# A single filler as 256 keys of both heads in one PSUM bank, with a TensorE wait between its halves, and singles at the units' first steps

## The chip, the cores and the metric

One Trainium2 chip, one core. The metric is device time of one execution in microseconds. The kernel before takes 1504.08 us in the median of three runs (1503.17 to 1506.13).

## The reference

Two attentions over the same x (2048 rows, width 512), mixed row by row by a gate:

```python
g = _sigmoid((x * gate_w).sum(-1, keepdims=True))
a = _A_ref(x, A_wqkv, A_wo)            # 32 heads of 16, each row sees 8 rows, 2 apart, up to itself
b = _B_ref(x, B_wq, B_wk, B_wv, B_wo)  # 32 query heads of 16, one key and value head, all rows
return g * a + (1 - g) * b
```

B is the long part. Its weights B_wq and B_wk are scaled by 8, so its scores are large, and the softmax needs the true maximum of each query's 2048 scores before it takes exponentials.

## The kernel before

**Units and steps.** B is cut into 32 units of 512 queries and 4 heads (`NQB` x `NHG`). A unit has 16 steps, one for each 128 keys, and step `s` of the main loop (lines 1106 to 1155) belongs to unit `s // 16`; `kt` is the step within the unit. A step does this:

- `exp_pair` (L468) twice: two score matmuls (L473), one head on the lower 64 rows of the TensorE array and one on the upper 64, into the two banks of `eb[0]` or `eb[1]` (`pe` in the profile), and one exponential by ScalarE (L475) of the 128 x 1024 scores.
- `weighted` (L480): four heads' exponentials of the step before times the values, into the bank `po` (L483), on all 128 rows.

**Fills.** The maxima come from a second pass over the same scores, spread between the steps of earlier units: for each of a unit's 8 groups of 128 queries and head pairs, and each quarter of the keys (512), two matmuls of 62 rows (`max_mm`, L324) and a maximum over the keys by VectorE into the tile `mx`. The list `slots` holds these items in order; an item counts as two halves, one a head, and a unit has `NF // NU` = 64 of them. `filled` (L329) counts a unit down; at zero it reduces `mx` once more (L334) and sends the maxima to the rows 62 and 63 of the unit's queries, so the scores that the exponentials see are already shifted.

- A **pair** (`fill_pair`, L339) does an item at once: two matmuls into the two banks of `m2` (`pm` in the profile), one reduction of 128 x 1024 (L344).
- A **single** (`fill_one`, L348) does half an item, one head: one matmul of 512 keys into the bank `m1` (`ps`), one reduction of 128 x 512 (L355).

**Order.** The order on every engine is the order in which the Python code emits instructions. It is steered by a planner: `clk` is its time on TensorE, ScalarE and VectorE, `free` the time at which each bank is free, `T_R` to `T_TTR` (L45) its costs, `after` (L86) adds one. In a step the usual order is first scores, pair, single, second scores, weighted sum. `fill_ready` (L853) takes a fill if its bank is free by the planner's clock; `singles(s)` (L849) lets singles in while the pairs of the steps ahead can't do the rest; singles are left out at a unit's first step (`kt` zero, L1145), where `finish_a` (L495) also has VectorE transpose `po` (L497). Where a unit's maxima would come too late, `pause` (L863) does fills with the exponentials' banks while no step goes on.

**Around it.** Before the main loop, the projections run with fills between them (`stream`, L689). Three times `out_phase` (L728) projects four output rows of 128; the last four are done by the generator `spread` (L776): its matmuls (L812) go into `m2`, four pairs a step, once all fills are done, and each row's sum is taken out by ScalarE (L829) and VectorE (L831) into `parts`. After the last step the tail (L1163 to L1188) normalises the last unit, multiplies it by its part of the output weights and adds `parts`. GpSimd computes attention A and sets the `mx` tiles.

Of the kernel before, what the change touches and what calls it, by code (L numbers as in the profile page):

```python
# [13 lines left out]
P = 128  # L14
# [34 lines left out]
def gated_mix_kernel(ctx, tc, xt, wa, wk, wq, wo_a, wo_b, out):  # L49
# [20 lines left out]
    def home(v):  # L70

        return (v % NB, v - NB) if v < 2 * NB - 2 else ((v - NB) % (NB - 2), v - NB + 2)
# [13 lines left out]
    def after(eng, ready, dur):  # L86
        clk[eng] = max(clk[eng], ready) + dur
        return clk[eng]
# [213 lines left out]
    half = []  # L302
# [4 lines left out]
    def fillable():  # L307
        return bool(half) or bool(slots) and slots[0][0] < len(stacked) and stacked[slots[0][0]] <= clk["pe"]

    def unit_tile(v):  # L310
        for x in (v, v + 1) if pe else (v,):
            if x < NU and x not in left:
                mx[x] = wp.tile([P, 2, 2, 4, 4], F32, name="mx", bufs=3)
                if pe:
                    nc.gpsimd.memset(mx[x], -FMAX)
                    charge(250)
                else:
                    nc.scalar.activation(mx[x].rearrange("p b i t k -> p (b i t k)"), ident[:, 0:64], AF.Identity, scale=0.0, bias=mk[:, 6:7])
                left[x] = NF // NU
        return mx[v]  # L320
# [3 lines left out]
        nc.tensor.matmul(dst, qst[home(v)[0]][b:b + 62, pr, t * P:(t + 1) * P], kst[b:b + 62, kc * 512:(kc + 1) * 512], start=True, stop=True)  # L324

    def to_go():
        return 2 * len(slots) + len(half)

    def filled(v, n):  # L329
        left[v] -= n  # L330
        if not left[v]:
            ms = wp.tile([P, 2, 2, 8], F32, name="ms")
            m = mx.pop(v).rearrange("p b i t k -> p b (i t) k")
            nc.vector.tensor_reduce(ms, m.unsqueeze(2).to_broadcast([P, 2, 2, 8, 4]), AX.X, ALU.max)  # L334
            mt = wp.tile([P, 32], F32, name="mt")
            nc.vector.transpose(mt, ms.rearrange("p b x y -> p (b x y)"))
            tasks.append((after("dve", 0, 0.66) + (2.0 if kcd and not pe else 0.1), shift_a, (v, mt)))

    def fill_pair(dst, key):  # L339
        v, pr, t, kc = slots.pop(0)  # L340
        m = unit_tile(v)
        for odd in range(2):
            max_mm(dst[:, odd, :], v, pr, t, kc, odd)
        nc.vector.tensor_reduce(m[:, :, pr, t, kc], dst, AX.X, ALU.max)  # L344
        free[key] = after("dve", after("pe", 0, T_R) + T_LAT, T_RED2) + 0.08
        filled(v, 2)

    def fill_one(dst=m1, key="m1"):  # L348
        if not half:
# [115 lines left out]

    pe, pexp, exped = [], {}, {}

    def exp_pair(s, pr, other=False):  # L468
        bank, key = (m2, "m2") if other else (eb[pr], f"e{pr}")
        u, kt = divmod(s, NJ)  # L470
        for odd in range(2):
            b = 64 * odd
            nc.tensor.matmul(bank[:, odd, :], kst[b:b + 64, kt * P:(kt + 1) * P], qst[home(u)[0]][b:b + 64, pr, :], start=True, stop=True)  # L473
        e = px.tile([P, 2, 512], F32, name="pexp", bufs=6)
        nc.scalar.activation(e, bank, AF.Exp, scale=SCALE)  # L475
        free[key] = after("act", after("pe", free[key], T_R) + T_LAT, T_EXP)
        exped[s] = free[key]
        pexp[s, pr] = e

# [296 lines left out]
    def spread(js, n):  # L776

        m = 3 * (C + n)

        def turn_all(j):  # L780
            bank = m1
            for c in range(C):
                nc.tensor.transpose(bank[:, c * P:(c + 1) * P], oa[c // 2][:, j, c % 2 * P:(c % 2 + 1) * P], ident)
            after("pe", 0, 0.7)
            own = p2[0].tile([P, C, P], F32, name="raw", bufs=1)
            nc.scalar.activation(own, bank.rearrange("p (c q) -> p c q", c=C), AF.Copy)
            after("act", clk["pe"] + T_LAT, 0.6)
# [12 lines left out]
        parts_a(js[0], turn_all(js[0]))  # L800
        yield 3.0
        while slots or half:
            yield 1.0
        for j in js:
            nxt = j + 1 if j != js[-1] else None
            items = []
            for i in range(m):
                items = items or out_items(j, n)
                st, mv = items[i]
                for b in range(2):  # L810
                    h = slice(64 * b, 64 * b + 64)
                    nc.tensor.matmul(m2[:, b, :], st()[h], mv[h], start=(i == 0), stop=(i == m - 1))  # L812
# [16 lines left out]
            nc.scalar.activation(parts[j], m2[:, 1, :], AF.Copy)  # L829
            after("dve", after("act", clk["pe"] + T_LAT, 0.5), 0.7)  # L830
            nc.vector.tensor_add(parts[j], m2[:, 0, :], parts[j])  # L831
            if nxt:
                parts_a(nxt, raw)
            yield 1.5
        done.add("last")

    def spread_some(k):
# [13 lines left out]
        return 2 * max(0, 16 * (NU - 1) - 16 - s) + PER_ROW * max(0, NJ - 4 - outs) < to_go()  # L851

    def fill_ready(key, slack):  # L853
        if fillable() and free[key] <= clk["pe"] + slack:
            clk["pe"] = max(clk["pe"], free[key])
            if key == "m1":
                fill_one()
            elif half and (not slots or half[0][0] < slots[0][0] or slots[0][0] >= len(stacked)):
                fill_one(m2[:, 0, :], "m2")
            elif slots:  # L860
                fill_pair(m2, "m2")

    def pause(most):  # L863
        n = 0
        while n < most and slots and fillable():
            key = min(("e0", "e1", "m2"), key=lambda k: free[k])
            clk["pe"] = max(clk["pe"], free[key])
            if half:
# [191 lines left out]
    def done_mm(at):  # L1060
# [45 lines left out]
    for s in range(NS + 1):  # L1106
# [11 lines left out]
        v = min(x[0][0] for x in (half, slots, [(NU,)]) if x)  # L1118
# [4 lines left out]
        order = (0, "m2", "m1", 1) if s > 1 else (1, "m2", 0, "m1") if s else ()  # L1123
        k, n = outs // 4, C - (outs >= NJ - 4)
        if outs == NJ - 4:
            if NU - 3 in shaped and not half and not singles(s) and not later_rows and "last" not in done:
                later_rows.append(spread(list(range(outs, NJ)), n))
            if short > 0 and steps < 2:
                pause(short)
# [8 lines left out]
        elif short > 0 and steps < 2:  # L1138
            pause(short)

        for which in order:
# [18 lines left out]
    assert not slots and not half and not hooks and not tasks and "last" in done, (len(slots), len(hooks), len(tasks), outs)  # L1160


    for x in range(8):  # L1163
# [2 lines left out]
    for x in range(2):  # L1166
# [51 lines left out]
```

## Time and profile before

| | us |
|---|---|
| median of the runs | 1504.08 |
| the profiled execution | 1503.76 |
| its span | 1502.0 |
| TensorE busy | 1479.2 |
| ScalarE busy | 1285.7 |
| VectorE busy | 1188.4 |
| GpSimd busy | 1024.8 |

How to read the lines below: in the timeline, the columns are the start in us from the span's start, the time, the engine, the kernel's line, the operation, the tiles written and read, their shapes and how many instructions are merged in the row; in brackets stands the engine's idle time before it and what ended it. PE is TensorE's matmuls, PEld its weight loads, DVE is VectorE, ACT ScalarE, POOL GpSimd. In a row of groups, "| 196.8, 398 |" is the busy time in us and the mean of one in ns. In a row of windows the stretch and its length come first, then busy time and (count) of the line asked for; in a row for all engines these stand for PE, PEld, DVE, ACT and POOL in this order; the granted TensorE clock (1.00 is full) follows. A matmul's row runs from its start to the modelled arrival of its last column; the next one on the same rows can start before that end.

### The profile page before, as it was taken

To read this page: it belongs to the slowest core of one execution; us is meant where nothing else is said; L and a number is where in the kernel's file an instruction comes from. 1 tells how busy PE (TensorE), PEld (TensorE's weight loads), DVE (VectorE), ACT (ScalarE), POOL (GpSimd) and SP (SyncE) were. 2 spreads that over 40 slices of the span, in tenths; PEclk is the share of its full clock that TensorE was granted. 3 is DMA by queue.
4 is the path that set the end of the run, shared out by engine and by line. 5 is a ranking of instruction groups with operands and counts; after the bars stand their busy time and mean duration, and the time that the engine had idled before them with its cause. 6 is when DMAs were issued, how large, how long until landed. Compare 5 with 4: busy or idle time off the path is not lost.

```text
span 1502.0 us, 29449 instructions
## 1 busy us (share of the span) xinstructions
PE 1479.2 (98%) x11020; PEld 710.5 (47%) x11020; DVE 1188.4 (79%) x1814; ACT 1285.7 (86%) x1672; POOL 1024.8 (68%) x1806
## 2 busy tenths in 40 slices
PE   9999999999999999999999999999999999999998
PEld 6899888433333333333733345333333463333343
DVE  6976666788888888888788888888888888888801
ACT  5568988899999999999899988999989889999785
POOL 7876988788888888988988799788897130111021
PEclk9999999999999999999999999999999999999999
DMA  6754223121120211211212112021120000000000
GB/s 219 212 147 143 76 87 117 33 83 46 60 84 12 73 58 41 70 41 41 69 41 70 41 41 87 12 70 41 41 76 16 12 30 12 2 1 2 1 2 28
DMA packets 44287, 87.75 MB, mean 58 GB/s; under 512 B 9520, under 2 KB 25952, under 8 KB 39920
## 3 DMA queue, kind: packets, MB, share of 16 engines
q1 hardware_dynamic: 37136, 46.89, 10.3%
q0 software_dynamic: 6432, 37.94, 7.5%
q8 instruction: 86, 1.41, 0.4%
q10 hardware_dynamic: 576, 1.05, 0.2%
q14 instruction: 57, 0.47, 0.1%
HBM read 59.02 MB, written 26.30 MB: 57 GB/s over the span
## 4 chain that ended last, share of the span: by engine, by line
PE 91%; ACT 5%; DVE 2%; issue 1%; DMA 0%; POOL 0%; SPq 0%; DVEq 0%; ACTq 0%; POOLq 0%
PE po L483 33%; PE pe L473 25%; PE pe L1057 8%; PE pm L324 8%; PE ps L324 5%; PE pe L740 4%; PE pm L409 2%; ACT dd L419 2%; ACT pexp L475 1%; PE ps L409 1%; PE pm L812 1%; PE po L409 1%; PE pe L183 1%; DMA xraw<-xt 0%; DVE mx L344 0%
## 5 line engine op out<-in xcount | busy, mean ns | idle before, releaser
L475 ACT ACTIVATE pexp<-pe 128x1024 f32<-128x1024 f32 x1021 | 987.3, 1023 | 106.0 <-PE pe L473 103.6
L344 DVE TENSOR_REDUCE mx<-pm 128x2 f32<-128x1024 f32 x508 | 620.0, 1221 | 147.4 <-PE pm L324 139.6
L483 PE MATMUL po<-pexp,vst 128*32 128x512 f32 x4096 | 546.6, 606 | 0.0
L473 PE MATMUL pe<-qst,kst 64*128 64x512 f32 x1914 | 520.4, 455 | 5.6 <-DVE mx L344 2.9
L473 PEld LDWEIGHTS pe<-qst,kst 64*128 64x128 f32 x1914 | 213.3, 184 | 424.6 <-ACT pexp L475 410.2
L355 DVE TENSOR_REDUCE mx<-ps 128x1 f32<-128x512 f32 x446 | 303.1, 680 | 2.1 <-PE ps L324 2.1
L324 PE MATMUL pm<-kst,qst 62*128 62x512 f32 x968 | 196.8, 398 | 2.9 <-DVE mx L344 2.1
L543 POOL TENSOR_TENSOR pr<-aext 128x256 f32<-128x256 f32 x256 | 182.6, 741 | 3.4 <-DMA aext<-ad 3.1
L324 PE MATMUL ps<-kst,qst 62*128 62x512 f32 x422 | 177.3, 420 | 0.5 <-DVE mx L355 0.3
L603 POOL TENSOR_TENSOR oa<-oa,av 128x256 f32<-128x256 f32 x224 | 164.5, 734 | 14.9
L483 PEld LDWEIGHTS po<-pexp,vst 128*32 128x32 f32 x4096 | 80.6, 108 | 174.5 <-issue 166.6
L600 POOL TENSOR_TENSOR av<-aext,lg 128x256 f32<-128x256 f32 x224 | 139.7, 623 | 12.5
L324 PEld LDWEIGHTS ps<-kst,qst 62*128 62x128 f32 x422 | 77.5, 184 | 68.3 <-DVE mx L355 64.9
L1057 PE MATMUL pe<-wah,xl 64*128 64x384 f32 (+1 forms) x504 | 108.9, 338 | 0.0
L419 ACT ACTIVATE dd<-pm 128x512 f32<-128x512 f32 x166 | 92.0, 608 | 19.6 <-PE pm L409 9.5
L1057 PE MATMUL pe<-wah,xh 64*128 64x384 f32 (+1 forms) x504 | 108.6, 337 | 0.0
L1057 PE MATMUL pe<-wal,xh 64*128 64x384 f32 (+1 forms) x504 | 108.3, 337 | 0.0
L429 DVE CUSTOM_DVE_ANT_0 dd<-ps,dd 128x512 f32<-128x512 f32 x83 | 57.4, 692 | 58.4 <-PE ps L409 25.4
L324 PEld LDWEIGHTS pm<-kst,qst 62*128 62x128 f32 x968 | 93.2, 187 | 8.0 <-DVE mx L344 3.4
L509 POOL TENSOR_TENSOR rl<-rl,gate_t 128x16 f32<-128x16 f32 x31 | 6.9, 222 | 118.2 <-DVE rl L503 118.1
L549 POOL TENSOR_TENSOR tr<-pr 128x512 f32<-128x512 f32 x64 | 81.7, 1277 | 4.1
L549 POOL TENSOR_TENSOR tr<-tr 128x256 f32<-128x256 f32 (+1 forms) x128 | 72.5, 567 | 9.0
(215 smaller groups left out, 1908.1 us busy)
## 6 DMA issues: line engine op xcount, KB each, us to landing
aext<-ad POOLq DMA_DIRECT2D x32, 1056.0 KB, 5.5
ad<-stage SPq DMA_DIRECT2D x32, 384.0 KB
qst<-qd SPq DMA_DIRECT2D x60, 128.0 KB
xraw<-xt SPq DMA_DIRECT2D x16, 256.0 KB
qd<-qhi SPq DMA_DIRECT2D x16, 256.0 KB
qd<-qlo SPq DMA_DIRECT2D x16, 256.0 KB
qst<-qd SPq DMA_DIRECT2D x60, 64.0 KB
qst<-ml SPq DMA_DIRECT2D x216, 2.0 KB
```

Source lines behind the costliest of these rows:

```text
L324: nc.tensor.matmul(dst, qst[home(v)[0]][b:b + 62, pr, t * P:(t + 1) * P], kst[b:b + 62, kc * 512:(kc + 1) * 512], start=True, stop=True)
L344: nc.vector.tensor_reduce(m[:, :, pr, t, kc], dst, AX.X, ALU.max)
L355: nc.vector.tensor_reduce(m[:, odd, pr, t, kc:kc + 1], dst, AX.X, ALU.max)
L419: nc.scalar.activation(dd[0][:, odd], m2[:, odd, :], AF.Abs)
L473: nc.tensor.matmul(bank[:, odd, :], kst[b:b + 64, kt * P:(kt + 1) * P], qst[home(u)[0]][b:b + 64, pr, :], start=True, stop=True)
L475: nc.scalar.activation(e, bank, AF.Exp, scale=SCALE)
L483: nc.tensor.matmul(po[32 * i:32 * i + 32, :], vst[:, kt, :], pexp[s, i // 2][:, i % 2, :], start=(kt == 0), stop=(kt == NJ - 1))
L543: nc.gpsimd.tensor_mul(pr[:, k], q, e[:, o:o + NH, AC:2 * AC])
L549: nc.gpsimd.tensor_add(nx, cur[:, :, 0:n], cur[:, :, n:2 * n])
L600: nc.gpsimd.tensor_mul(av, e[:, o:o + NH, 2 * AC:].rearrange("p j (h d) -> p j h d", d=DH), lg[:, w].unsqueeze(3).to_broadcast([P, NH, AG, ...
L603: nc.gpsimd.tensor_add(ao, ao, av)
L1057: nc.tensor.matmul(front[2 if x == last else x % 2][0][:, b, :n], l[h], r[h], start=(i == 0), stop=(i == 3 * C - 1))
```

## The change

- A single becomes 256 keys of **both** heads in the one bank `m1` (`fill_apart`): even head in columns 0 to 255, odd head in 256 to 511. The two matmuls use different halves of the array and the same bank. They stand around the second pair of scores of the step: first half on the lower rows, the scores of the odd head (upper rows), the scores of the even head (lower rows), then an instruction without work that waits until the first half is in the bank, then the second half on the upper rows. One reduction takes both maxima.
- Since an item has then two quarters of keys in one place of `mx`, a second tile `mb` takes the upper 256 keys; it is set by GpSimd as `mx` is, and `filled` joins the two with one `tensor_max`. An item begun so is ended by a second such single or by `fill_rest`, which does 256 keys of both heads in `m2` or in another pair of banks.
- Singles are let in at the units' first steps. Where half an item is open, or an item's unit has no `mb`, the old form stays.
- The planner counts 0.2 us more for scores with such a single, where before the single had `T_R` (0.23).
- `spread` may begin with up to 9 halves left; between its rows VectorE alone empties `m2`; the last row's add stands behind the first transposes of the tail, and one subtraction of the tail goes from GpSimd to VectorE. At the end of the projections a stretch without new pairs (`ended`) begins four matmuls sooner.

```diff
     def unit_tile(v):
-        for x in (v, v + 1) if pe else (v,):
+        for x in (v, v + 1):
...
                 if pe:
+                    mb[x] = pe[0].tile([P, 2, 2, 4, 4], F32, name="mb", bufs=3)
+                    nc.gpsimd.memset(mb[x], -FMAX)
+                    charge(250)
...
     def to_go():
-        return 2 * len(slots) + len(half)
+        return 2 * len(slots) + len(half) + len(quarter)
...
-            m = mx.pop(v).rearrange("p b i t k -> p b (i t) k")
+            m = mx.pop(v)
+            if v in mb:
+                nc.vector.tensor_max(m, m, mb.pop(v))
+            m = m.rearrange("p b i t k -> p b (i t) k")
...
+    def fill_apart(scores):
+
+        if not quarter:
+            v, pr, t, kc = slots.pop(0)
+            quarter.extend([(v, pr, t, kc, 0), (v, pr, t, kc, 1)])
+        v, pr, t, kc, x = quarter.pop(0)
+        m = mb[v] if unit_tile(v) is not None and x else mx[v]
+        ks = slice(kc * 512 + x * 256, kc * 512 + x * 256 + 256)
+        for odd in range(2):
+            b = 64 * odd
+            if odd:
+                scores(1)
+                scores(0)
+                nc.tensor.keepalive_nop([nc.tensor.lower_ap(m1[:, 0:256])])
+            nc.tensor.matmul(m1[:, 256 * odd:256 * odd + 256], qst[home(v)[0]][b:b + 62, pr, t * P:(t + 1) * P], kst[b:b + 62, ks], start=True, stop=True)
+        nc.vector.tensor_reduce(m[:, :, pr, t, kc], m1.rearrange("p (b k) -> p b k", b=2), AX.X, ALU.max)
+        filled(v, 1)
...
-    def exp_pair(s, pr, other=False):
+    def exp_pair(s, pr, other=False, apart=False):
...
+        if apart:
+            fill_apart(scores)
+        else:
+            scores(0)
+            scores(1)
         e = px.tile([P, 2, 512], F32, name="pexp", bufs=6)
         nc.scalar.activation(e, bank, AF.Exp, scale=SCALE)
-        free[key] = after("act", after("pe", free[key], T_R) + T_LAT, T_EXP)
+        at = after("pe", free[key], T_R + 0.2 * apart)
+        free[key] = after("act", at + T_LAT, T_EXP)
+        if apart:
+            free["m1"] = after("dve", at + T_LAT, T_RED1) + 0.08
...
-            nc.scalar.activation(parts[j], m2[:, 1, :], AF.Copy)
-            after("dve", after("act", clk["pe"] + T_LAT, 0.5), 0.7)
-            nc.vector.tensor_add(parts[j], m2[:, 0, :], parts[j])
             if nxt:
+                nc.vector.tensor_copy(parts[j], m2[:, 1, :])
+                nc.vector.tensor_add(parts[j], m2[:, 0, :], parts[j])
                 parts_a(nxt, raw)
-            yield 1.5
+                after("dve", clk["pe"] + T_LAT, 1.4)
+                yield 1.5
+            else:
+                nc.scalar.activation(parts[j], m2[:, 1, :], AF.Copy)
...
-        if x == last - 1 and i == 3 * C - 2:
+        if x == last - 1 and i == 3 * C - 6:
             ended.add(1)
...
-            if NU - 3 in shaped and not half and not singles(s) and not later_rows and "last" not in done:
+            if NU - 3 in shaped and to_go() <= 9 and not later_rows and "last" not in done:
                 later_rows.append(spread(list(range(outs, NJ)), n))
...
             elif which == "m1":
-                if not later_rows and (kt or not s) and singles(s):
-                    fill_ready("m1", M1S)
+                if not later_rows and singles(s):
+                    if half or slots and not quarter and slots[0][0] in left and slots[0][0] not in mb:
+                        fill_ready("m1", M1S)
+                    elif (quarter or fillable()) and free["m1"] <= clk["pe"] + M1S and s < NS:
+                        apart = True
             elif s < NS:
-                exp_pair(s, which % 2 or which // 2, which == 2)
+                if apart and which:
+                    clk["pe"] = max(clk["pe"], free["m1"])
+                exp_pair(s, which % 2 or which // 2, which == 2, apart and which > 0)
...
-        nc.gpsimd.tensor_sub(tl[:, 1], own, tl[:, 0].bitcast(F32))
+        (nc.vector if x else nc.gpsimd).tensor_sub(tl[:, 1], own, tl[:, 0].bitcast(F32))
         tls.append(tl)
+        if not x:
+            nc.vector.tensor_add(parts[NJ - 1], m2[:, 0, :], parts[NJ - 1])
```

More of the change, by code (lines that the diff above doesn't have):

```diff
@@ L301, in gated_mix_kernel @@
     slots += [(v, pr, t, kc) for v in range(2, NU) for pr in range(2) for t in range(4) for kc in range(4)]
-    half = []
+    half, quarter, mb = [], [], {}
     free = {"m2": 0.0, "m1": 0.0, "e0": 0.0, "e1": 0.0, "po": 0.0}
@@ L346, in fill_pair, with fill_rest @@
         filled(v, 2)
+    def fill_apart(scores):
[14 more added lines that the diff above has]
+        filled(v, 1)
+    def fill_rest(dst, key):
+        v, pr, t, kc, x = quarter.pop(0)
+        m = mb[v] if x else mx[v]
+        for odd in range(2):
+            b = 64 * odd
+            c = kc * 512 + x * 256
+            nc.tensor.matmul(dst[:, odd, 0:256], qst[home(v)[0]][b:b + 62, pr, t * P:(t + 1) * P], kst[b:b + 62, c:c + 256], start=True, stop=True)
+        nc.vector.tensor_reduce(m[:, :, pr, t, kc], dst[:, :, 0:256], AX.X, ALU.max)
+        free[key] = after("dve", after("pe", 0, T_R) + T_LAT, T_RED1) + 0.08
+        filled(v, 1)
     def fill_one(dst=m1, key="m1"):
@@ L466, in gated_mix_kernel, with scores @@
     pe, pexp, exped = [], {}, {}
-    def exp_pair(s, pr, other=False):
+    def exp_pair(s, pr, other=False, apart=False):
         bank, key = (m2, "m2") if other else (eb[pr], f"e{pr}")
         u, kt = divmod(s, NJ)
-        for odd in range(2):
+        def scores(odd):
             b = 64 * odd
             nc.tensor.matmul(bank[:, odd, :], kst[b:b + 64, kt * P:(kt + 1) * P], qst[home(u)[0]][b:b + 64, pr, :], start=True, stop=True)
+        if apart:
[3 more added lines that the diff above has]
+            scores(1)
         e = px.tile([P, 2, 512], F32, name="pexp", bufs=6)
         nc.scalar.activation(e, bank, AF.Exp, scale=SCALE)
-        free[key] = after("act", after("pe", free[key], T_R) + T_LAT, T_EXP)
+        at = after("pe", free[key], T_R + 0.2 * apart)
+        free[key] = after("act", at + T_LAT, T_EXP)
+        if apart:
+            free["m1"] = after("dve", at + T_LAT, T_RED1) + 0.08
         exped[s] = free[key]
@@ L801, in spread @@
         yield 3.0
-        while slots or half:
+        while slots or half or quarter:
             yield 1.0
@@ L853, in fill_ready @@
     def fill_ready(key, slack):
-        if fillable() and free[key] <= clk["pe"] + slack:
+        if (fillable() or quarter) and free[key] <= clk["pe"] + slack:
             clk["pe"] = max(clk["pe"], free[key])
@@ L857, in fill_ready @@
                 fill_one()
+            elif quarter and (later_rows or not slots or quarter[0][0] < slots[0][0]):
+                fill_rest(m2, "m2")
             elif half and (not slots or half[0][0] < slots[0][0] or slots[0][0] >= len(stacked)):
                 fill_one(m2[:, 0, :], "m2")
-            elif slots:
+            elif slots and fillable():
                 fill_pair(m2, "m2")
@@ L864, in pause @@
         n = 0
-        while n < most and slots and fillable():
+        while n < most and (quarter or slots and fillable()):
             key = min(("e0", "e1", "m2"), key=lambda k: free[k])
             clk["pe"] = max(clk["pe"], free[key])
+            if quarter:
+                fill_rest({"e0": eb[0], "e1": eb[1], "m2": m2}[key], key)
+                n += 1
+                continue
             if half:
@@ L1117, in gated_mix_kernel @@
                     assert pause(4)
-        v = min(x[0][0] for x in (half, slots, [(NU,)]) if x)
+        v = min(x[0][0] for x in (half, quarter, slots, [(NU,)]) if x)
         need = left.get(v, NF // NU)
@@ L1139, in gated_mix_kernel @@
             pause(short)
+        apart = False
         for which in order:
@@ L1159, in gated_mix_kernel @@
         run_pool()
-    assert not slots and not half and not hooks and not tasks and "last" in done, (len(slots), len(hooks), len(tasks), outs)
+    assert not slots and not half and not quarter and not hooks and not tasks and "last" in done, (len(slots), len(hooks), len(tasks), outs)
     for x in range(8):
```

## The prediction

> **What bounds the kernel now.** I read the page's first line, the busy shares and the chain that ended last; then the timeline of single steps of the main loop; then counts by stretch.
>
> ```profile
> span 1502.0 us, 29449 instructions
> PE 1479.2 (98%) x11020; PEld 710.5 (47%) x11020; DVE 1188.4 (79%) x1814; ACT 1285.7 (86%) x1672; POOL 1024.8 (68%) x1806
> ...
> PE 91%; ACT 5%; DVE 2%; issue 1%; DMA 0%; POOL 0%; SPq 0%; DVEq 0%; ACTq 0%; POOLq 0%
> ```
>
> TensorE carries 91% of the chain, so the end moves with what TensorE's own queue costs. The profiled execution took 1503.76 us (1502.0 of it span), 0.3 under the median of the three runs, 1504.08; I sum against 1503.8 and add nothing for the difference. The timeline's TensorE rows of one step, between two weighted sums:
>
> ```profile
> 603.18 1.07 PE L483 MATMUL po<-pexp,vst 128*32 128x512 f32 x8
> ...
> 605.36 1.07 PE L483 MATMUL po<-pexp,vst 128*32 128x512 f32 x8
> 606.35 0.50 PE L473 MATMUL pe<-qst,kst 64*128 64x512 f32 x2
> 606.70 0.40 PE L324 MATMUL pm<-kst,qst 62*128 62x512 f32 x2
> 606.93 0.40 PE L324 MATMUL ps<-kst,qst 62*128 62x512 f32 x1
> 606.94 0.63 PE L473 MATMUL pe<-qst,kst 64*128 64x512 f32 x2
> 607.50 0.64 PE L483 MATMUL po<-pexp,vst 128*32 128x512 f32 x4
> ```
>
> From one weighted sum to the next: 2.18 and 2.14 us, 2.16 in the mean. The parts of the second: 0.99 weighted sum, 0.35 first scores, 0.23 the pair, and 0.57 for the single with the second scores (606.93 to 607.50). One of those scores runs beside the single (606.94) on the other 64 rows; the last follows it. That 0.57 is what the change rebuilds. A step without a single:
>
> ```profile
> 611.82 1.06 PE L483 MATMUL po<-pexp,vst 128*32 128x512 f32 x8
> 613.71 1.06 PE L483 MATMUL po<-pexp,vst 128*32 128x512 f32 x8
> ```
>
> 1.89 us, so a single costs 0.27. The singles' and the pairs' reductions in the main loop, from the windows by line, and the reductions of two steps:
>
> ```profile
> 274.20:1416.50 1142.30, 288.23 (x424) 1.00 0.13 42
> ...
> 274.20:1416.50 1142.30, 583.94 (x479) 1.00 0.13 42
> ```
>
> ```profile
> 604.96 1.23 DVE L344 TENSOR_REDUCE mx<-pm 128x2 f32<-128x1024 f32 x1
> 606.10 0.68 DVE L355 TENSOR_REDUCE mx<-ps 128x1 f32<-128x512 f32 x1
> 607.14 1.23 DVE L344 TENSOR_REDUCE mx<-pm 128x2 f32<-128x1024 f32 x1 [0.36 <-PE pm L324]
> ```
>
> ```profile
> 606.46 0.19 PEld L324 LDWEIGHTS pm<-kst,qst 62*128 62x128 f32 x2
> 606.83 0.18 PEld L324 LDWEIGHTS ps<-kst,qst 62*128 62x128 f32 x1 [0.18 <-DVE mx L355]
> ```
>
> 424 singles in 479 steps that have a pair. There is a second, hidden limit. The single's bank is free at 606.78 (606.10 + 0.68); its weights load 0.05 later, at 606.83, and its matmul starts 0.10 after that. From the pair of the step before (2.18 earlier, 604.52) to the earliest single is 2.42 us, and a single stands 0.24 behind its own pair: **VectorE lets two neighbouring steps average no less than about (2.18 + P)/2**, where P is TensorE's own step (2.14 now). That is why steps alternate between 2.14 and 2.18. Whatever TensorE gains per step, half is given back here.
>
> **The change part by part.** *The rebuilt single.* Now: one matmul of 512 columns on 64 rows, then scores. After: first half (256 columns, lower rows), scores(1) on the upper rows, scores(0) on the lower, a wait until the first half has been written, second half (256 columns, upper rows). Keys times heads per single are the same, so the number of singles is too. Column time alone would fall: each half of the array streams 512 + 256 columns instead of one of them streaming 1024. But the wait stands in TensorE's queue ahead of the second half's weight load, and behind it stand the weighted sum, the next scores and the next pair. How long a short matmul takes, start to end:
>
> ```profile
> L324 PE MATMUL pm<-kst,qst 62*128 62x512 f32 x968 | 196.8, 398 | 2.9 <-DVE mx L344 2.1 <-ACT pexp L475 0.8
> L1057 PE MATMUL pe<-wah,xl 64*128 64x384 f32 x376 | 81.0, 335 | 0.0
> ...
> L646 PE MATMUL pe<-ident,oa 64*128 64x64 f32 x96 | 5.1, 224 | 0.0
> ```
>
> 398, 335 and 224 ns for 512, 384 and 64 columns: 256 columns take about 0.29. (The Trainium skill, TensorE: Matmul & The Clock Gate, Single matmul latency, gives (398 + N)/2.4 ns: 272 for 256, by which the sum below would come out 8 us lower; the trace's 398 at 512 stands above its 379.) For telling the sequencer there are two lags:
>
> ```profile
> 606.96 1.94 ACT L475 ACTIVATE pexp<-pe 128x1024 f32<-128x1024 f32 x2 [0.24 <-PE pe L473]
> ```
>
> The pair ended at 607.10 and VectorE began at 607.14: 0.04. The first scores ended at 606.85 and ScalarE, which waits for two things, began at 606.96: 0.11. A wake-up of TensorE took 0.05 (above). I take 0.05 for the wake-up and another 0.04, the shorter of the two lags, for the waiting instruction itself, which no row shows (bounds 0 and 0.15, a little over the longer lag). Then 0.10 from weight load to streaming, as at 606.83 to 606.93. From a 512-column matmul to the weighted sum behind it is 0.33 (the last scores end at 606.94 + 0.63, so begin about 0.40 earlier, at 607.17, and the sum at 607.50); with 256 columns 0.11 less: 0.22. Sum, from the first half to the weighted sum: 0.29 + 0.05 + 0.04 + 0.10 + 0.22 = **0.70**, against 0.57 now. The scores in between would let it start at about 0.49 (0.11 of columns, 0.05, 0.33), so they hide only part. So P = 2.14 + 0.13 = 2.27; VectorE's loop (2.18) no longer holds, and there is no alternation. Per single 2.27 - 2.16 = +0.11: 424 x 0.11 = **+47 us**. Bounds: with the instruction free and the weights already there, 0.29 + 0.05 + 0.22 = 0.56, P = 2.13, mean 2.16, 0 us; with 0.15 for it, 0.81, P = 2.38, +93 us. A gain would need the first half to be known earlier than its 0.29 and a wake-up; since the profile's matmul ends are modelled I keep that as a rival.
>
> *Exponentials.* The second scores end earlier, but ScalarE does the two exponentials in 1.94 of a longer step; nothing follows. *Reduction.* Same 512 elements per lane, 0.68 as L355; it starts behind the pair's reduction, after the second half is there. *One tensor_max a unit and a second memset:*
>
> ```profile
> L334 DVE TENSOR_REDUCE ms<-mx 128x32 f32<-128x128 f32 x32 | 9.2, 286 | 1.1
> ```
>
> Some 0.3 on VectorE by the nearest row, covered by its idle 0.36 a step, and on GpSimd, 68% busy and off the chain. Without that cover the tensor_max would cost 0.3 x 30 units (479 steps by 16) = 9 us.
>
> *Singles at the units' first steps.*
>
> ```profile
> 613.59 1.23 DVE L344 TENSOR_REDUCE mx<-pm 128x2 f32<-128x1024 f32 x1 [0.31 <-PE pm L324]
> ...
> 614.85 0.72 DVE L497 STREAM_TRANSPOSE tt<-po 128x512 f32<-128x512 f32 x1
> ```
>
> The bank `po` must be transposed before the next unit's weighted sum may start. Here the pair's reduction began 0.12 ahead of the unit's last weighted sum (613.71); in a step 0.38 longer (2.27 for 1.89) it begins 0.50 ahead. Then 1.14, the single's 0.68 and 0.72 are done 2.04 after that sum, and the next starts at 2.27: no stall, while a single one or two steps on comes late and may be skipped. At most one more single for each of some 27 units (30 less the three whose first step holds an output phase), so the list is empty up to 9 steps sooner (three halves a step); the number is the same. Bounds 0 and, if the transpose holds that sum up by a third of the single's 0.68, 0.2 x 27 = 5 us: I take 0.
>
> *The end.* Now the last fills are done in a pause:
>
> ```profile
> 1416.45 1.06 PE L483 MATMUL po<-pexp,vst 128*32 128x512 f32 x8
> ...
> 1422.13 0.80 PE L473 MATMUL pe<-qst,kst 64*128 64x512 f32 x2 [2.90 <-DVE mx L344]
> ...
> 1423.71 1.94 PE L483 MATMUL po<-pexp,vst 128*32 128x512 f32 x8
> ...
> 1426.72 1.28 PE L483 MATMUL po<-pexp,vst 128*32 128x512 f32 x8
> ```
>
> ```profile
> 1416.50:1425.00 8.50, 5.29 (x30) 1.81 (x29) 7.02 (x9) 3.27 (x4) 0.00 (x0) 0.73 0.01 3
> ```
>
> 10.3 us for three steps that need 5.7, partly because TensorE's granted clock fell to 0.73: 4.6 go, and some 9 halves that were done in it become singles or pairs (9 x 0.38 = 3.4 at most, a single's new price). The later rows begin sooner, and their bank is emptied by VectorE alone:
>
> ```profile
> 1447.03 0.60 ACT L829 ACTIVATE part<-pm 128x512 f32<-128x512 f32 x1
> ...
> 1447.67 0.69 DVE L831 TENSOR_TENSOR part<-pm,part 128x512 f32<-128x512 f32 x1 [1.92 <-ACT part L829]
> ...
> 1448.41 0.97 PE L812 MATMUL pm<-woh,own 64*128 64x512 f32 x6 [0.25 <-DVE part L831]
> ```
>
> TensorE waits 0.25 there, three times, and VectorE's two operations (some 1.4) take about as long as now (1447.03 to 1448.36): 0 to -1.5. Starting earlier and the add moved past the last transposes: -1 to -3. The end together: -10 to +3, I take **-5**, which is what the pause and the row start show.
>
> Sum: 1503.8 + 47 - 5 = **1546**.
>
> **The rivals.** *Weights pulled ahead of the wait:* 0.10 less, 0.60; P = 2.17, the mean with VectorE's loop 2.175, 0.015 x 424 = 6, less 5: **1505**. For it: weight loads run ahead of their matmuls (606.46 for 606.70). Against: the load at 606.83 came only after VectorE's signal, so a wait holds loads back. (The Trainium skill, same page, Architectural detail: the array is 16x 32x32, says that TensorE's queue can pull weight loads ahead of matmuls in flight; whether ahead of a wait no run here shows.) *The wait is over when TensorE reaches it:* the modelled ends are late and the signal comes while scores(0) still streams; the single with the scores takes 0.53 instead of 0.57, P = 2.10, VectorE's loop makes the mean 2.14: -0.02 x 424 = -8, less 5: **1491 to 1499**, say 1495. It decides from 0.56 downwards. Against it are the 0.29 and the 0.05. *The waiting instruction is dear* (0.15): 1503.8 + 93 - 5 = **1592**; halfway, at 0.10, P = 2.33 and **1571**. *The change hardly comes to pass*, its conditions keeping most singles in the old form: 0 - 5, about **1499**; against it, only units whose tiles were made before the main loop keep the old form.
>
> **How the numbers follow.** Forecast 1546 (1530 to 1560): 0.58. Dear instruction, above 1560: 0.13. Weights ahead, 1500 to 1515: 0.10, half of it slower by over 0.2% and half within. Hidden wait: 0.15. Hardly used: 0.04, half of it faster. 0.2%, 3 us, is about what a measurement of this kernel can tell from no change. Slower: 0.58 + 0.13 + 0.05 = 0.76; within: 0.05 + 0.02 = 0.07; faster: 0.15 + 0.02 = 0.17. The range takes in the weights-ahead case, the upper half of the hidden wait and half of the dear one: 1495 to 1578, which leaves out some 0.15.
>
> **What would show it.** In the changed trace the second half starts 0.4 to 0.5 after the first and the weighted sum about 0.7 after it; a step with a single takes 2.25 to 2.30 without alternating, one without still 1.9; the idle time before the second half's weight load is put down to TensorE; VectorE's idle time before the pair's reduction grows from 0.36 to 0.45; the pause near 1416 is gone. A second half at 0.35 or earlier, or steps at 2.15, would make the prediction wrong; so would stalls of the weighted sum at the units' first steps, or a pause that is longer than now.

## The result, and the profile after

The changed kernel takes 1578.02 us in the median of four runs (1575.47 to 1579.29), the kernel before beside it 1504.64 (1503.17 to 1506.13): the ratio is 1.0482 (with a 95% interval of [1.0465, 1.0498]), 73 us more. The forecast was 1546 (1530 to 1560), 42 us more; 1578 is the upper end of the wide range that it gave for all its cases together.

The page of the kernel after: the span, the busy engines and the engines' shares of the chain that ended last.

```profile
span 1576.2 us, 31136 instructions
...
PE 1546.0 (98%) x11442; PEld 815.4 (52%) x11442; DVE 1207.1 (77%) x1843; ACT 1280.4 (81%) x1660; POOL 1024.3 (65%) x1828
...
PE 85%; DVE 4%; POOL 4%; ACT 3%; issue 2%; DMA 2%; SPq 1%; DVEq 0%; POOLq 0%; ACTq 0%
```

TensorE is busy 98% of a span that is 74 us longer. A busy row here holds waiting too: rows run to the modelled end of the columns, and the wait lies under the row of the first half or of the scores. So the step itself has to be read. TensorE's rows of one step with a single, in the timeline after:

```profile
652.48 1.07 PE L529 MATMUL po<-pexp,vst 128*32 128x512 f32 x8
653.48 0.50 PE L510 MATMUL pe<-qst,kst 64*128 64x512 f32 x2
653.81 0.40 PE L327 MATMUL pm<-kst,qst 62*128 62x512 f32 x2
654.05 0.28 PE L368 MATMUL ps<-kst,qst 62*128 62x256 f32 x1
654.05 0.51 PE L510 MATMUL pe<-qst,kst 64*128 64x512 f32 x2
654.47 0.38 PE L368 MATMUL ps<-kst,qst 62*128 62x256 f32 x1
654.78 1.07 PE L529 MATMUL po<-pexp,vst 128*32 128x512 f32 x8
657.08 0.64 PE L529 MATMUL po<-pexp,vst 128*32 128x512 f32 x4
```

The weighted sums start at 652.48, 654.78 and 657.08: 2.30 and 2.30 us, where before they stood 2.18 and 2.14 apart in turn. The first half (654.05) is followed 0.42 later by the second (654.47), and that 0.31 later by the weighted sum: 0.73 from the first half to the weighted sum, where the single and its scores took 0.57. The weight load of the second half, in the same stretch, and the row of the waits in the main loop that groups such loads (us in total, times, longest):

```profile
654.47 0.18 PEld L368 LDWEIGHTS ps<-kst,qst 62*128 62x128 f32 x1 [0.24 <-PEq L367]
```

```profile
PEld ps L368 <- PEq L367: 92.9, 387, 0.4
```

The idle time ahead of that load is put down to TensorE's own queue, to line 367: the waiting instruction. It comes 387 times with 0.24 each in the mean.

From the starts of all 512 weighted sums, taken from the two traces, follows an account of the main loop (the 511 distances between them, in us):

| steps | before: number, median, sum | after: number, median, sum |
|---|---|---|
| with a pair and a single | 394, 2.15, 853.7 | 413, 2.30, 964.8 |
| with a pair alone | 63, 1.90, 120.5 | 42, 1.90, 79.6 |
| others (output phases, last rows, steps over 5 us) | 54, -, 240.2 | 56, -, 243.4 |
| together | 1214.4 | 1287.8 |

The 73.4 more are 413 x (2.30 - 2.15) = 62 in the usual step with a single; 8 in longer ones among them (964.8 - 413 x 2.30 = 14.9 above the median, before 853.7 - 394 x 2.15 = 6.6); 3 in the other steps; and nothing in the exchange of 19 steps (19 x 2.15 = 40.9, as many as the steps with a pair alone lost). Most of the long steps stand in two places. Two of them, 6.7 and 4.0 us long at 449.6 and 456.2, lie 6 us above the median together (the longer is among the other steps). Of those with a single and a pair, 18 begin within 2 us of a unit's last reduction (L340) and are more than 0.1 above the median: 9.1 us in all. The experiments below come back to both. The front and the tail around these steps differ by less than 3 us each.

### The profile page after: what moved, and what is told of

Read it like the earlier page. It is cut to its first block, busy times and chain, and to the rows that moved or that the text cites. A ratio compares the mean times of both kernels' runs of the same rounds, so it can differ in the third digit from the quotient of the medians.

```text
span 1576.2 us, 31136 instructions
## 1 busy us (share of the span) xinstructions
PE 1546.0 (98%) x11442; PEld 815.4 (52%) x11442; DVE 1207.1 (77%) x1843; ACT 1280.4 (81%) x1660; POOL 1024.3 (65%) x1828
## 4 chain that ended last, share of the span: by engine, by line
PE 85%; DVE 4%; POOL 4%; ACT 3%; issue 2%; DMA 2%; SPq 1%; DVEq 0%; POOLq 0%; ACTq 0%
PE po L529 30%; PE pe L510 21%; PE ps L368 10%; PE pm L327 7%; PE pe L1111 6%; PE pe L786 4%; PE pm L445 2%; DVE mx L350 2%; PE pm L858 1%; ACT dd L455 1%; PE ps L445 1%; POOL qlo L220 1%; POOL qraw L213 1%; PE po L445 1%; DVE mx L338 1%
## 5 line engine op out<-in xcount | busy, mean ns | idle before, releaser
L510 PE MATMUL pe<-qst,kst 64*128 64x512 f32 x1914 | 474.0, 449 | 7.1 <-ACT pexp L518 4.9
L510 PEld LDWEIGHTS pe<-qst,kst 64*128 64x128 f32 x1914 | 244.2, 184 | 426.8 <-ACT pexp L518 402.5
L368 PE MATMUL ps<-kst,qst 62*128 62x256 f32 x834 | 273.6, 328 | 2.9 <-issue 1.1
L368 PEld LDWEIGHTS ps<-kst,qst 62*128 62x128 f32 x834 | 153.2, 184 | 120.0 <-PEq L367 92.9
L369 DVE TENSOR_REDUCE mx<-ps 128x2 f32<-128x512 f32 x211 | 143.6, 680 | 0.8 <-PE ps L368 0.8
L369 DVE TENSOR_REDUCE mb<-ps 128x2 f32<-128x512 f32 x206 | 140.6, 682 | 0.0
```

The source lines that it names most:

```text
L368: nc.tensor.matmul(m1[:, 256 * odd:256 * odd + 256], qst[home(v)[0]][b:b + 62, pr, t * P:(t + 1) * P], kst[b:b + 62, ks], start=True, stop ...
L369: nc.vector.tensor_reduce(m[:, :, pr, t, kc], m1.rearrange("p (b k) -> p b k", b=2), AX.X, ALU.max)
```

## The experiments

My theory was the forecast's: the waiting instruction stands in TensorE's queue, and the weight load behind it can't run ahead. The rivals: the two short matmuls cost by themselves; the data of the first half come late, so that the wait is long whatever carries it; the rest of the change (first steps, `tensor_max`, the end) costs more than counted. A ratio below is against runs of the kernel before that were made beside the run; their medians were 1506.10, 1504.94 and 1505.91.

**The split alone, and the split with the wait.** Both are the kernel before with the single's matmul cut into two of 256 keys around the second scores, both on the same rows, so that no wait is needed. The second kernel has the waiting instruction all the same. The core of the edit (the planner's part is left out here):

```diff
...
+        for x in range(2):
+            if x:
+                scores(1 - odd)
+                scores(odd)
+                nc.tensor.keepalive_nop([nc.tensor.lower_ap(m1[:, 0:256])])
+            c = kc * 512 + x * 256
+            nc.tensor.matmul(m1[:, 256 * x:256 * x + 256], qst[home(v)[0]][b:b + 62, pr, t * P:(t + 1) * P], kst[b:b + 62, c:c + 256], start=True, stop=True)
...
```

The first kernel is without the line of `keepalive_nop`.

> The kernel before, with one edit: a single's matmul of 512 keys of one head is split into two of 256 keys, one ahead of and one behind the second pair of scores, both on the same half of the array, so nothing has to be waited for. Theory (the wait is the cost): from the first half to the weighted sum 0.12 + 0.23 + 0.11 + 0.10 = 0.56 us, as the unsplit single's 0.57; time 1500 to 1512 us. Rival (short matmuls, one more weight load and the new order of the scores are the cost): most of the +0.15 us a single is there without a wait; 1540 to 1570 us.

> As split_free, and between the halves the instruction without work that waits until the first half is in its bank, as in the changed kernel; it differs from split_free in this instruction alone. Theory: the second half starts about 0.42 us after the first, the weighted sum 0.73 after it, a step with a single takes 2.30 us and does not alternate; +0.145 x some 415 = +60: 1555 to 1575 us. Rival (the split is the cost): the same time as split_free within 8 us.

Measured: 1513.17 (1511.74 to 1513.74), ratio 1.0045 [1.0030, 1.0060], for the split, 1 us above what was expected, and 1568.27 (1565.13 to 1573.84), ratio 1.0416 [1.0391, 1.0441], with the wait. TensorE's rows and weight loads of a step of the first:

```profile
661.41 0.28 PE L373 MATMUL ps<-kst,qst 62*128 62x256 f32 x1
661.42 0.50 PE L491 MATMUL pe<-qst,kst 64*128 64x512 f32 x2
661.76 0.27 PE L373 MATMUL ps<-kst,qst 62*128 62x256 f32 x1
661.97 1.06 PE L507 MATMUL po<-pexp,vst 128*32 128x512 f32 x8
```

```profile
661.26 0.34 PEld L491 LDWEIGHTS pe<-qst,kst 64*128 64x128 f32 x2
661.53 0.19 PEld L373 LDWEIGHTS ps<-kst,qst 62*128 62x128 f32 x1
```

and of the second:

```profile
656.43 0.28 PE L374 MATMUL ps<-kst,qst 62*128 62x256 f32 x1
656.55 0.39 PE L492 MATMUL pe<-qst,kst 64*128 64x512 f32 x1
656.86 0.38 PE L374 MATMUL ps<-kst,qst 62*128 62x256 f32 x1
657.17 0.64 PE L508 MATMUL po<-pexp,vst 128*32 128x512 f32 x4
```

```profile
656.85 0.18 PEld L374 LDWEIGHTS ps<-kst,qst 62*128 62x128 f32 x1 [0.24 <-PEq L372]
```

Without the wait the second half's weights load at 661.53, 0.23 ahead of their matmul, and the step from first half to weighted sum is 0.56, against 0.57 before the change. With it the load stands at 656.85 and the matmul at 656.86: its row is 0.38 long instead of 0.27, the load being part of it now, and the sum comes 0.74 after the first half, against 0.73 in the changed kernel. One instruction without work, with the wait that it carries, costs 55 us over 394 steps, 0.14 a step; the split costs 7. The rival of the two short matmuls falls.

**The wait twice.** The changed kernel with the waiting instruction a second time: the data are there when the second one's turn comes.

```diff
                 nc.tensor.keepalive_nop([nc.tensor.lower_ap(m1[:, 0:256])])
+                nc.tensor.keepalive_nop([nc.tensor.lower_ap(m1[:, 0:256])])
```

> The changed kernel with the waiting instruction written twice; the second finds its signal there already. If the instruction itself takes TensorE's sequencer 0.05 to 0.10 us: +20 to +43 us, 1598 to 1621 us. If only the waiting counts: within 8 us of the changed kernel's 1578.

Measured: 1632.94 (1631.60 to 1634.54), ratio 1.0845 [1.0827, 1.0863], above what was expected by either theory. Rows and load of one step:

```profile
654.14 0.28 PE L369 MATMUL ps<-kst,qst 62*128 62x256 f32 x1
654.15 0.51 PE L511 MATMUL pe<-qst,kst 64*128 64x512 f32 x2
654.72 0.38 PE L369 MATMUL ps<-kst,qst 62*128 62x256 f32 x1
655.03 1.07 PE L530 MATMUL po<-pexp,vst 128*32 128x512 f32 x8
```

```profile
654.71 0.18 PEld L369 LDWEIGHTS ps<-kst,qst 62*128 62x128 f32 x1 [0.39 <-PEq L368]
```

The idle time before the load grows from 0.24 to 0.39, and the median step from 2.30 to 2.46. So a second instruction costs 0.15 of a step though no data are late for it. In the trace's semaphore records (a semaphore is a counter that one instruction adds to and another waits for) each of the two has an event of its own, 0.15 apart, and the load follows 0.10 behind the last. The first waits for the semaphore of the first half; it adds to another one, for which the second waits, and the load waits for that same one. So the second isn't free of waiting: it waits for the first. What costs is the instruction with the signal that it passes on; an instruction that waits for nothing was not tried. Still, this falls on the side of the price and against late data: from the end of the first half to the load, with one instruction, there are 0.14 (654.05 + 0.28 to 654.47 in the changed kernel), of which 0.04 pass before its event and 0.10 after it. An estimate from these rows: with the load right behind those 0.04, the weighted sum would come 0.28 + 0.04 + 0.10 + 0.21 = 0.63 after the first half, so of the 0.18 between the two split kernels (0.56 and 0.74) some 0.07 are the wait for the data and the other 0.11 the instruction.

**One tile for the maxima.** The changed kernel with both halves' maxima in one tile, so that the last reduction of a unit reads 8 values instead of 4 and there is no `tensor_max`; an open quarter is closed ahead of each output phase.

```diff
...
-                    mb[x] = pe[0].tile([P, 2, 2, 4, 4], F32, name="mb", bufs=3)
-                    nc.gpsimd.memset(mb[x], -FMAX)
...
+                    both = pe[0].tile([P, 2, 2, 4, 4, 2], F32, name="mb", bufs=2)
+                    mx[x], mb[x] = both[:, :, :, :, :, 0], both[:, :, :, :, :, 1]
...
+                    nc.gpsimd.memset(both, -FMAX)
...
-                nc.vector.tensor_max(m, m, mb.pop(v))
...
```

> The changed kernel with the two halves of the keys in one tile of maxima, so that the unit's last reduction reads 8 values instead of 4 and the tensor_max is gone (an open half is closed ahead of each output phase, and one wider memset takes the place of two). Theory that the tensor_max, which took 0.54 to 1.32 us while GpSimd worked, holds the next pair up: 8 to 10 us less, 1567 to 1571 us. Rival (the singles at the units' first steps fill VectorE's queue there): within 3 us of 1578.

Measured: 1568.95 (1568.12 to 1572.11), ratio 1.0420 [1.0405, 1.0436]: 9 us less than the changed kernel. What the `tensor_max` did there, in the groups, at 1066 and at 1502:

```profile
L338 DVE TENSOR_TENSOR mx<-mx,mb 128x64 f32<-128x64 f32 x24 | 13.3, 555 | 0.8
```

```profile
1067.39 1.30 POOL L595 TENSOR_TENSOR tr<-pr 128x512 f32<-128x512 f32 x1
1067.45 1.32 DVE L338 TENSOR_TENSOR mx<-mx,mb 128x64 f32<-128x64 f32 x1
...
1069.61 1.20 POOL L595 TENSOR_TENSOR tr<-tr 128x256 f32<-128x256 f32 x2
...
1069.83 1.22 DVE L350 TENSOR_REDUCE mx<-pm 128x2 f32<-128x1024 f32 x1
...
1071.10 0.50 PE L327 MATMUL pm<-kst,qst 62*128 62x512 f32 x2 [0.87 <-DVE mx L350]
```

```profile
1502.27 0.23 DVE L338 TENSOR_TENSOR mx<-mx,mb 128x64 f32<-128x64 f32 x1
```

The same instruction takes 0.23 us at 1502.27, where GpSimd does nothing, and 1.32 at 1067.45, where a GpSimd operation that had begun 0.06 earlier ends at 1068.69, 0.08 before it. VectorE is 1.1 us late, its reduction of the pair too, and the next pair's matmul waits 0.87 for its bank. The other 22 are of the same two kinds: 9 of the 24 take 0.22 to 0.23, and each of the 15 longer ones ends 0.08 to 0.09 after the end of a GpSimd `tensor_tensor` that had begun before it or ran right behind one that had. (The Trainium skill, SBUF — State Buffer, Who interferes with whom, says that a VectorE instruction with two inputs in SBUF contends with a GpSimd instruction that reads SBUF, whichever starts first blocking the other; these rows agree.) In the kernel with one tile the longer reduction stands in the place of both, and it has one length; of the long steps near a unit's last reduction, 18 with 9.1 us in the changed kernel, 3 with 0.8 us are left:

```profile
L342 DVE TENSOR_REDUCE ms<-mb x24: 419/420/422, 388.1 to 1495.2; 128x32 f32<-128x256 f32 x24
```

**The first steps, alone and taken out.** One kernel is that before with singles at the units' first steps, the other the changed kernel without them.

```diff
-                if not later_rows and (kt or not s) and singles(s):
+                if not later_rows and singles(s):
```

> The kernel before with singles let in at the units' first steps, and no other edit. The prediction's term was 0 to +5: within 3 us of the kernel before, since as many singles are done and the list is empty sooner. Rival (VectorE's queue with the unit's last reductions, the transpose and one more single holds the next pair up): +4 to +12 us.

> The changed kernel with singles left out again at the units' first steps. If the new singles there cost what the prediction took, 0 to 5 us: 1573 to 1578 us. Rival (they are the cause of most of the 12 us that the changed kernel's stalled steps hold beyond its usual step): 1565 to 1571 us.

Measured: 1511.68 (1506.68 to 1512.20), ratio 1.0031 [1.0018, 1.0045], alone; 1573.89 (1570.59 to 1575.01), ratio 1.0452 [1.0438, 1.0467], taken out: by the ratios 4 to 5 us either way, where the forecast had none (the medians differ by 6.7 and 4.1). Waits of the main loop in the first of the two:

```profile
PEld po L483 <- DVE tt L497: 10.5, 27, 1.0
...
PEld pm L324 <- DVE mx L344: 2.9, 14, 0.4
```

At 27 units the weighted sum's weights stand behind the transpose of `po`, once in the kernel before; VectorE is late by the single's reduction, and two steps on the pair finds its bank taken 14 times: the third step of a unit, one without a single, takes 2.00 in the median instead of 1.90 (32 x 0.1 = 3). This is the forecast's upper bound, and in the range of the expectation's rival. In the changed kernel, whose steps are longer, the wait for the transpose doesn't show. What shows there is in the same places as the `tensor_max`: without the first steps' singles the long steps near a unit's last reduction are 15 with 4.1 us, where the changed kernel has 18 with 9.1. The `tensor_max` and the single's reduction stand in one queue there, so their 9 and 4 us overlap and don't add up.

**The end alone, in two forms.** The kernel before with the edits of the last bullet of the change; in the second form without the one at the end of the projections.

```diff
-        if x == last - 1 and i == 3 * C - 6:
+        if x == last - 1 and i == 3 * C - 2:
```

> The kernel before with the change's edits at the ends alone (later rows begin with up to 9 halves left, VectorE alone empties their bank, the last add and one subtraction of the tail moved, the projections' stretch without pairs begun sooner); the singles are as before. The prediction's term was -5 (-10 to +3): 1495 to 1501 us. Rival from the changed kernel's trace, where a pause of 5.7 us and a main loop that begins 2.6 us later still stand: -2 to +1, 1502 to 1506 us.

> The kernel before with the change's edits at the ends but one: the projections' stretch without pairs begins where it did (the condition with 3 * C - 2 is back). Theory: that edit shifts the planner's order so that one load of the output weights is issued late and ScalarE waits 5.4 us for it in its queue, as the trace of the run with all of the ends shows at 441 to 446 us; without it the ends are worth their -3 to -5: 1499 to 1503 us. Rival (the other edits cost what was measured): 1507 to 1510 us.

Measured: 1508.59 (1505.09 to 1511.77), ratio 1.0022 [1.0014, 1.0031], with it, above both of its expectations, and 1501.92 (1499.87 to 1507.91), ratio 0.9978 [0.9967, 0.9989], without it. The timeline of the first form:

```profile
446.35 0.63 ACT L81 ACTIVATE woh<-os 128x512 fp32r<-128x512 f32 x1 [5.37 <-DMA os<-wo_b]
...
447.94 0.79 PE L473 MATMUL pe<-qst,kst 64*128 64x512 f32 x2 [5.65 <-ACT pexp L475]
```

ScalarE stands 5.37 us in its queue before a part of the output weights that is still on its way, and the exponentials behind it hold TensorE for 5.65. The other order of work that follows from the earlier `ended` puts this operation ahead of its load's landing. In the changed kernel it is 3.57 and 3.53 us, at 452; these are the two long steps from 449.6 on. So the end was worth -3, where the forecast had -5, and the projections' edit took back 7. The -3 don't come from the pause. In the second form the weighted sums around it stand 7.25 us apart, in the kernel before 7.26 (1416.45 to 1423.71):

```profile
1416.32 1.06 PE L483 MATMUL po<-pexp,vst 128*32 128x512 f32 x8
...
1423.57 1.93 PE L483 MATMUL po<-pexp,vst 128*32 128x512 f32 x8
```

There it is 0.1 us ahead of the kernel before, at its end 3.9: the gain lies in the later rows and the tail.

**The single behind the scores.** The forecast's hidden limit (VectorE's loop, which gives back half of what TensorE gains) can be tried without any wait: the kernel before with the second scores ahead of the single.

```diff
-        order = (0, "m2", "m1", 1) if s > 1 else (1, "m2", 0, "m1") if s else ()
+        order = (0, "m2", 1, "m1") if s > 1 else (1, "m2", 0, "m1") if s else ()
```

> The kernel before with one edit: in a step the single stands behind the second scores, not ahead of them. Theory of the prediction (VectorE's two reductions hold the single's bank until 2.42 us after the pair of the step before; with the single 0.24 us later in its step that no longer binds): steps with a single stop alternating and take TensorE's own 2.14 us, 0.02 x 415 = 8 us less, 1494 to 1498 us. Rival (TensorE's queue alone sets the step): within 2 us of the kernel before.

Measured: 1499.51 (1499.33 to 1501.23), ratio 0.9965 [0.9954, 0.9977]: 0.35% faster than the kernel before, though between its two expectations. TensorE's rows of two steps:

```profile
412.25 1.07 PE L483 MATMUL po<-pexp,vst 128*32 128x512 f32 x8
413.24 0.50 PE L473 MATMUL pe<-qst,kst 64*128 64x512 f32 x2
413.58 0.40 PE L324 MATMUL pm<-kst,qst 62*128 62x512 f32 x2
413.82 0.40 PE L473 MATMUL pe<-qst,kst 64*128 64x512 f32 x2
414.06 0.40 PE L324 MATMUL ps<-kst,qst 62*128 62x512 f32 x1
414.38 1.07 PE L483 MATMUL po<-pexp,vst 128*32 128x512 f32 x8
...
416.50 1.06 PE L483 MATMUL po<-pexp,vst 128*32 128x512 f32 x8
```

The single is asked for 0.24 later in the step, its bank is free by then, and the steps are 2.13 and 2.12 long with no alternation. The waits of the single's weight load for its bank in the main loop (274 to 1416 us), in the kernel before and in this one (us in total, times, longest):

```profile
PEld ps L324 <- DVE mx L355: 68.0, 323, 0.4
```

```profile
PEld ps L324 <- DVE mx L355: 1.5, 4, 0.8
```

The limit was where the forecast put it. The gain is 5 us and not 8 (394 x 0.02): the planner lets singles into 418 steps now instead of 394, and some 40 of them take 2.3 to 2.4. **With the end's edits** as well (without that of the projections):

> The kernel before with the single behind the second scores (as single_last) and the ends as in ends_late. If the two add: 1499.5 - 3 = 1495 to 1498 us, faster than both kernels. If the earlier end of the fills only moves idle steps to the end: 1499 to 1501 us.

Measured: 1501.08 (1498.43 to 1505.59), ratio 0.9971 [0.9960, 0.9983], where 1495 to 1498 was expected if they add: the two gains don't add up.

## Why the prediction was right in its direction and 32 us short

The result lies outside 1530 to 1560, in the part that the forecast called the dear instruction (chance 0.13), and at the very end of the range that takes in all cases. The direction was right for its reason. That the time stayed as near as it did is in part luck, as the terms show.

- **TensorE's own queue sets the end**: right. The step with a single grew by 0.15, and 413 x 0.15 = 62 of the 73 us are there.
- **The rebuilt single, 0.70 from first half to weighted sum**: the mechanism right, the size 0.03 short; the trace has 0.73. First half 0.28 (0.29 taken), until the instruction's event 0.04 (0.05), from there to the load 0.10, load 0.10, last columns to the sum 0.21 (0.22). Three terms were each 0.01 too large, which hid half of a miss of 0.06 in the fourth. The mis-sized term is the waiting instruction itself: 0.04 by the shorter of two lags of other engines, inside bounds of 0 and 0.15; measured 0.10 with one, and 0.15 for a second. The forecast had one wake-up; by the semaphores there are two, that of the instruction and that of the load that waits for the instruction. The forecast chose the end of its bounds that lay nearer to the rows it had, and those were of engines woken by another, not of an instruction that passes TensorE's queue.
- **P = 2.27, no alternation, +0.11 per single**: the steps are 2.30, without alternation, +0.15 against a median of 2.15. Of the 0.04 between, 0.03 is P and 0.01 the reference, 2.16 from two steps where the median of all 394 is 2.15. 0.04 x 413 = 16 of the 32 us are here.
- **Weights ahead of the wait; the hidden wait**: fell. The load comes behind the instruction 387 times, and the split without the wait shows that it would else have run ahead. **The dear instruction** (0.10: 1571) came nearest. The signs that the forecast named for the step came out as named: 0.42, 0.73, 2.30, 1.90 without a single, the idle time put down to TensorE.
- **The `tensor_max`, 0.3 and covered**: wrong. 0.56 in the mean, up to 1.4, and not covered: 9 us. That the forecast gave the same price for the case without cover is luck: it had 30 of 0.3, there are 24 of 0.56, 13.3 us in all. The nearest row, a reduction of 0.29, was of another kind: it reads one operand, this one two, beside a GpSimd that is 65% busy.
- **First steps, 0**: 4 to 5, its upper bound; in the changed kernel they lie within the `tensor_max`'s 9.
- **The end, -5**: -3 for the end's own edits, but not from the pause, of which the forecast let 4.6 go (for up to 3.4 spent elsewhere). Its reading of the pause was off, too: from 1416.45 to 1426.72 there are two steps, not three, so 6.5 us more than the 3.8 that they need, not 4.6. And the projections' edit, which the forecast did not price, put a wait for a load into ScalarE's queue: together +3. The pause is not gone, it is 5.7 us between two weighted sums (1496.29 to 1502.01); the row of the scores that end it, in the timeline after:

```profile
1500.23 0.50 PE L510 MATMUL pe<-qst,kst 64*128 64x512 f32 x2 [2.22 <-DVE mx L350]
```

By single kernels 1504.6 + 62 (split and wait) + 9 + 4 + 3 = 1583 against 1578.0; with the first steps' 4 inside the 9 it is 1579. The forecast's 32 us go to the step with a single (16), the `tensor_max` with the first steps (9) and the end (8).

Open stay four things. A matmul of line 368 stands 1.12 us without a releaser that the profile shows:

```profile
922.60 0.38 PE L368 MATMUL ps<-kst,qst 62*128 62x256 f32 x1 [1.12 <-issue]
```

Why some 40 of the steps with the single behind the scores take 2.3 to 2.4 was not traced. How much of the waiting instruction's 0.10 would go if the load didn't wait for its signal is not known: no kernel leaves that out. And the changed kernel without an instruction that waits was not tried; the wait is there to settle the order in which the two halves write the one bank.

## What to carry to other kernels

An instruction that waits, put between two matmuls of one queue, costs more than the wait: here 0.10 us from its event to the weight load behind it, 0.15 for a second one, and the load doesn't run ahead any more. So it belongs where TensorE has slack, or the two writers belong in two banks, as the pair's two matmuls have them. Before taking a duration from a like row, look at the number of operands and at what the neighbour engine does in that moment. The order that asked for a bank later won 5 us for one line, where the larger change lost 73.

## What the runs showed of the hardware

- A TensorE instruction without work that waits for TensorE's own matmul: 0.14 us from the matmul's end to the next weight load, 0.15 more for a second one that waits for the first one's signal alone.
- A VectorE `tensor_tensor` of 128 x 64 with both operands in SBUF: 0.22 to 0.23 us in 9 of 24, six of them with GpSimd idle; in the other 15 up to 1.41, ending 0.08 to 0.09 behind the end of a GpSimd `tensor_tensor`; the pair's reduction kept its length beside one (1.22 at 1069.83 above, with GpSimd at work from 1069.61 on).
- The front of the program, unchanged in most of these kernels, ends between 274.0 and 279.1 us in their profiled executions. Part of it is the granted clock; the windows by engine of the kernel before and of the split without the wait (the column behind the last bracket is the clock):

```profile
20.00:60.00 40.00, 37.50 (x279) 28.57 (x279) 32.21 (x41) 21.08 (x32) 31.91 (x27) 1.00 0.61 171
```

```profile
20.00:60.00 40.00, 37.52 (x267) 29.34 (x267) 31.39 (x40) 20.20 (x31) 30.56 (x26) 0.96 0.57 157
```

40 us at 0.96 are 1.6 us, so differences of 3 us between two profiles say nothing; the terms above come from the steps or from medians.
